# Attention and a gated feed-forward on one core: the planner's DMA account, the fillers' rule, a third score buffer and a fixed draw

## The chip, the cores and the metric

The kernel runs on one core of a Trainium2 chip. A core has five engines with an instruction stream of their own, which runs in order: TensorE (PE, matrix products; its weight loads show as PEld), VectorE (DVE), ScalarE (ACT), GpSimd (POOL) and SyncE (SP, which here only starts DMA transfers). The metric is the device time of one execution in microseconds (us). Three timed runs of the kernel before gave 817.39 us in the median, 816.01 to 819.08.

## The reference

Four sequences of 448 tokens, 12 heads of width 64, fp32. Scores are mixed over heads before the softmax and the attention weights after it; what comes out goes, per token, through a layer of 768 to 2048 to 768 with the gate h * clip(h + 3, 0, 6) / 6.

```python
scores = scale * np.matmul(q, k.transpose(0, 1, 3, 2))
scores = np.einsum('bhij,hg->bgij', scores, w_pre)
scores = scores - np.max(scores, axis=-1, keepdims=True)
attn = np.exp(scores)
attn = attn / (np.sum(attn, axis=-1, keepdims=True) + 1e-09)
attn = np.einsum('bhij,hg->bgij', attn, w_post)
out = np.matmul(attn, v)                     # then x: (1792, 768)
h = x @ w_in
g = h * np.clip(h + 3.0, 0.0, 6.0) / 6.0
y = g @ w_out
```

## The kernel before

The queries of one sequence are taken in blocks m of 60 (8 blocks in each of 4 sequences, 32 in all). For a block, `scores` (L433) multiplies queries and keys of two head pairs at a time, three times (p = 0, 1, 2), each into a pair of PSUM banks. ACT copies the result to a buffer `s` in SBUF (L458; in the first two blocks ACT and DVE copy a half each, L455 and L456), and SP sends each `s` in four transfers (L465) to the tile T, where heads lie on partitions. T has two homes, `T_two` and `T_one`, for even and odd blocks.

`step` takes 10 queries in each of two halves from T: `pre` (L522, mixing over heads before the softmax) on PE, the row maximum `nb` on DVE (L530), the exponential on ACT (L531), the division on POOL (L540) and `post` (L559, mixing over heads after the softmax) on PE, whose result ACT and DVE put into `AR` (L570, L568). From step 24 on `post` works in split f16 (`eh`, `el`, L542, L543), before that in fp32 (the x32 and x64 rows). `av` (L604) multiplies AR by the values. `moe1` (L802) is the first product of the layer, with weights `wi` that DVE, ACT and POOL decode from 64-bit words (`w_in_item`, L650 to L720); the second product (L1076) is computed with seven block products P1 to P7 and runs from 618 us to the end. L840 are fillers: products of the identity that nobody reads.

No order is written by hand. The builder lists every piece of work with an engine, a duration, what it needs and a priority, and `Plan.schedule` plays it through on a modelled machine: each engine takes the ready piece of the lowest priority, PE staying with its kind of product for up to `stay`. What comes out is emitted as the static order of each engine. A transfer's landing is modelled by one rate (`DMA_RATE`) and a fixed lag. The priorities are shaken in 32 draws, with four values of `stay` each, and the plan with the earliest modelled end is taken. `filler` is asked at each PE piece with the modelled gap before it, and fills the gap with identity products while the modelled time is between 9 and 150.

Of the kernel before, what the change touches and what calls it, by code (L numbers as in the profile page):

```python
# [11 lines left out]
F16 = mybir.dt.float16  # L12
BF16 = mybir.dt.bfloat16
# [13 lines left out]
P = 128  # L27
# [4 lines left out]
CU = 60  # L32
# [27 lines left out]
TRIALS, JITTER = 32, 0.3  # L60


class Op:
    __slots__ = ("eng", "dur", "fn", "prio", "n", "succ", "order", "ready", "end", "bytes", "no", "mode", "takes", "then", "share")
# [49 lines left out]
class Plan:  # L114
# [3 lines left out]
    DMA_RATE = 345e3  # L118
# [3 lines left out]
    STAY = 3.0, 4.0, 6.0, 8.0  # L122
# [5 lines left out]
    def op(self, eng, dur, fn, r=(), w=(), prio=0.0, after=(), nbytes=0, mode=0, share=False):  # L128
        o = Op()
        o.share = share or eng == "POOL"  # L130
# [46 lines left out]
    def schedule(self, prio, stay):  # L177

        free, wait, ready, out = {}, {}, {}, []
        bw, mode, then = {"SP": 0.0, "ACT": 0.0}, None, None  # L180
        for o, n in zip(self.ops, self.counts):
            o.n, o.ready, o.end = n, 0.0, None
# [31 lines left out]
        while True:  # L214
# [19 lines left out]
            if e == "PE":  # L234
# [6 lines left out]
                o = x[2]  # L241
                for b in o.takes:
                    b.pool.take(b, self.HOP)
# [10 lines left out]
            if e == "PE" and self.filler:  # L254
                z = self.filler(free[e], t)
                if z is not None:
                    out.append((free[e], z))
# [18 lines left out]
    def run(self):  # L276
        self.link()
        best = None
        for k in range(TRIALS):
# [12 lines left out]
def body(ctx: ExitStack, tc: tile.TileContext, q4, kT, vj, wpre0, wpost0, ident0, w_in, w_out, outT):  # L292
# [37 lines left out]
    def pe(dur, fn, r, w, prio, after=(), mode=0):  # L330
        return plan.op("PE", dur, fn, r, w, prio, after, 0, mode)
# [7 lines left out]
    def bulk(nbytes, out, src, w, prio, after=()):  # L339
        q = BULK  # L340
        return plan.op(q, 0.5 if q == "SP" else 0.4, lambda: (SP if q == "SP" else ACT).dma_start(out(), src), [], w, prio, after, nbytes)
# [20 lines left out]
    def across(src, name, prio):  # L362

        slot = place(singles)
        top = const([1, 1], BF16, f"top_{name}")
# [10 lines left out]
    wpre0_f, wpre8 = (const([P, 64], F32, n, one) for n in ("wpre0_f", "wpre8"))  # L376
    wpost0_f, wpost_n = (const([P, HR], F32, n, one) for n in ("wpost0_f", "wpost_n"))
# [3 lines left out]
    def mixes():  # L381
        dma(32768, lambda: SP.dma_start(wpre0_f(), wpre0), [], [wpre0_f], -11)
        dma(30720, lambda: SP.dma_start(wpost0_f(), wpost0), [], [wpost0_f], -10.9)
        dma(32768, lambda: SP.dma_start(ident(), ident0), [], [ident], -10.8)
        pool(0.2, lambda: POOL.memset(ones(), 1.0), [], [ones], -20)
        dve(0.2, lambda: DVE.tensor_scalar(wpre8(), wpre0_f(), 1.0 / 8.0, None, op0=ALU.mult), [wpre0_f], [wpre8], -6)
        dve(0.3, lambda: amax(wst(), wpost0_f()), [wpost0_f], [wst], -6)
        wm, wmv = across(wst, "w", -5.5)

        def fin():  # L390
            pow2(wmv(), pw(), rw())
            DVE.tensor_scalar(wpost_n(), wpost0_f(), rw(), 2.0 ** 14, op0=ALU.mult, op1=ALU.mult)
# [3 lines left out]
        dve(1.0, fin, [(wm, 1), wpost0_f], [pw, rw, wpost_n, wpost_h, wpost_l], -3)  # L396
# [17 lines left out]
    AR = const([P, 17280], F16, "AR", apool)  # L414
    T_two = const([P, 6144], F16, "T_two", apool)
    T_one = const([P, 6, S], F32, "T_one", one)
    T_home = [lambda: T_two()[:, :5376].bitcast(F32).rearrange("p (t j) -> p t j", t=6), T_one]
# [4 lines left out]
    def a_view():  # L422
        return AR()[:, :].bitcast(F32).rearrange("p (x y) -> p x y", y=3 * CU)
# [13 lines left out]
    def scores(m, p, at):  # L437
# [7 lines left out]
        st = buf(wpool, [P, 2, S], F32, "x", f"s_{m}_{p}", X_BUFS) if m == 0 else buf(rot, [P, 2, S], F32, "s", f"s_{m}_{p}", 2)  # L445
# [750 lines left out]
```

## Time and profile before

| | |
|---|---|
| median of three runs | 817.39 us (816.01 to 819.08) |
| profiled execution | 814.55 us, of which the span is 812.6 us |
| busy PE, DVE, ACT, POOL | 97%, 74%, 65%, 46% of the span |
| fillers (L840) | 98 products |
| granted TensorE clock, mean | 0.994 |

A busy PE is not a PE at its peak: matmuls overlap, and a row of mean 259 ns may start every 96 ns. So what PE has to do is read from blocks of instructions in order of time (so many products from start to start) and what it loses from the gaps. The clock is given as a share of full speed: 1.0 is 2.4 GHz, 0.5 is 1.2 GHz.

### The profile page before, as it was taken

How to read it: one execution, taken by the hardware profiler on the slowest of the kernel's cores; microseconds unless marked ns; L12 is line 12 of the kernel's file. 1: busy time of each engine (PE TensorE's matmuls, PEld its weight loads, DVE VectorE, ACT ScalarE, POOL GpSimd, SP SyncE). 2: the span in 40 equal slices, each digit the busy share in tenths (PEclk: the TensorE clock that was granted, in tenths of full speed). 3: DMA queues.
4: the chain of work that ended last, by engine and by line, in shares of the span. 5: the costliest groups of instructions: out<-in, count | busy, mean ns of one | idle time of the engine just before them, and what ended most of it. 6: DMA issues, size and time to landing. Idle time of an engine off the chain costs nothing.

```text
span 812.6 us, 28101 instructions
## 1 busy us (share of the span) xinstructions
PE 791.4 (97%) x11634; PEld 639.0 (79%) x11634; DVE 599.9 (74%) x1185; ACT 529.6 (65%) x1043; POOL 376.7 (46%) x535
## 2 busy tenths in 40 slices
PE   8999988999999999999999998999999999999998
PEld 3466676577767788777786776678999999999998
DVE  4589898687669656987946888875479889888632
ACT  2477887778898767788767687885469584233200
POOL 3255799567789626677753676774310000000000
PEclk9799999999999999999999999999999999999999
DMA  6756671664455476667446855745459992754101
GB/s 217 235 162 210 186 232 54 191 219 144 142 153 177 121 247 214 201 196 243 137 151 213 274 170 178 223 123 180 139 169 363 339 329 72 226 154 143 35 19 52
DMA packets 100415, 146.96 MB, mean 181 GB/s; under 512 B 9824, under 2 KB 79552, under 8 KB 100288
## 3 DMA queue, kind: packets, MB, share of 16 engines
q1 hardware_dynamic: 100288, 145.17, 57.2%
q8 instruction: 91, 1.49, 0.8%
q14 instruction: 36, 0.29, 0.1%
HBM read 75.23 MB, written 31.20 MB: 131 GB/s over the span
## 4 chain that ended last, share of the span: by engine, by line
PE 62%; DMA 9%; ACT 8%; POOL 6%; DVE 6%; SPq 5%; issue 3%; ACTq 0%; POOLq 0%; DVEq 0%
PE single L1076 24%; PE single L802 16%; PE single L559 6%; PE pair L433 5%; SPq L465 4%; PE single L522 4%; PE single L604 4%; ACT e L531 3%; POOL el L543 2%; POOL e L540 2%; DMA T_two<-s 2%; PE single L840 2%; DMA wi<-in_w_in 2%; ACT s L458 2%; DMA wo<-in_w_out 2%
## 5 line engine op out<-in xcount | busy, mean ns | idle before, releaser
L802 PEld LDWEIGHTS <-wi 128*128 128x128 f16 x2304 | 213.0, 98 | 22.7 <-issue 14.1
L802 PE MATMUL single<-x,wi 128*128 128x208 f16 (+1 forms) x2304 | 227.6, 259 | 2.8 <-ACT e L531 2.2
L543 POOL TENSOR_TENSOR el<-e,eh 128x448 f16<-128x448 f32 x156 | 176.0, 1145 | 36.6 <-ACT eh L542 33.3
L540 POOL TENSOR_SCALAR e<-e,r 128x448 f32<-128x448 f32 x180 | 131.2, 739 | 34.0 <-DVE r L534 29.1
L1076 PEld LDWEIGHTS <-ws_P 128*128 128x128 f16 x1440 | 138.0, 98 | 0.0
L531 ACT ACTIVATE e<-single,nb 128x448 f32<-128x448 f32 x180 | 113.0, 636 | 22.7 <-DVE nb L530 22.6
L530 DVE TENSOR_REDUCE nb<-single 128x1 f32<-128x448 f32 x180 | 102.0, 614 | 17.7 <-PE single L522 17.1
L542 ACT ACTIVATE eh<-e 128x448 f16<-128x448 f32 x156 | 87.5, 579 | 23.5 <-POOL e L540 23.0
L458 ACT ACTIVATE s<-pair 128x896 f32<-128x896 f32 x90 | 82.4, 916 | 21.3 <-DMA T_two<-s 6.7
L433 PE MATMUL pair<-ks,qx 64*64 64x448 f32 x728 | 89.3, 560 | 3.7 <-ACT s L458 3.2
L815 ACT ACTIVATE g<-single,three,uh 128x208 f32<-128x208 f32 (+1 forms) x128 | 68.7, 539 | 37.1 <-PE single L802 35.5
L817 DVE SCALAR_TENSOR_TENSOR g<-g,six,single 128x208 f32<-128x208 f32 (+1 forms) x128 | 56.4, 442 | 44.8 <-ACT g L815 42.9
L604 PEld LDWEIGHTS single<-AR,v 128*64 128x64 f32 x1536 | 75.1, 137 | 13.4 <-issue 3.4
L559 PEld LDWEIGHTS <-eh 60*128 60x128 f16 x2496 | 66.5, 100 | 20.9 <-issue 19.5
L604 PE MATMUL single<-AR,v 128*64 128x120 f32 (+1 forms) x1536 | 80.4, 263 | 0.4 <-ACT e L531 0.4
L559 PE MATMUL single<-wpost_h,el 60*128 60x60 f16 x1248 | 72.4, 202 | 1.9 <-POOL el L543 1.9
L559 PE MATMUL single<-wpost_h,eh 60*128 60x60 f16 x1248 | 72.9, 202 | 0.5 <-DVE g L817 0.4
L559 PE MATMUL single<-wpost_l,eh 60*128 60x60 f16 x1248 | 72.5, 202 | 0.0
L533 POOL TENSOR_SCALAR sm<-sm 128x2 f32<-128x2 f32 (+1 forms) x92 | 21.8, 237 | 106.3 <-ACT e L531 101.4
L1076 PE MATMUL single<-gx_P,ws_P 128*128 128x224 f16 x720 | 69.3, 259 | 0.0
L559 PEld LDWEIGHTS <-el 60*128 60x128 f16 x1248 | 64.1, 101 | 2.5 <-POOL el L543 2.4
L568 DVE TENSOR_SCALAR AR<-single 128x480 f32<-128x480 f32 (+1 forms) x92 | 58.1, 639 | 9.6 <-PE single L559 9.2
(247 smaller groups left out, 1176.9 us busy)
## 6 DMA issues: line engine op xcount, KB each, us to landing
T_two<-s SPq DMA_DIRECT2D x192, 105.0 KB
T_one<-s SPq DMA_DIRECT2D x144, 105.0 KB
wi<-in_w_in SPq DMA_DIRECT2D x16, 768.0 KB
wo<-in_w_out SPq DMA_DIRECT2D x24, 512.0 KB
wsd_P<-WF SPq DMA_DIRECT2D x42, 256.0 KB
wP<-wsd_P SPq DMA_DIRECT2D x36, 256.0 KB
gd<-g SPq DMA_DIRECT2D x32, 240.0 KB
gd<-g SPq DMA_DIRECT2D x32, 208.0 KB
```

The costliest lines, as they stand in the source:

```text
L433: PE.matmul(at[u]()[cc * D:cc * D + D], q()[r, o:o + D], ks_[cc]()[r, pr % 3, :], start=True, stop=True)
L458: act(0.9, lambda: ACT.activation(st(), two()[:, :, :S], AF.Copy), ps, [(st, 0), (st, 1)], at + 0.5)
L530: dve(0.53, lambda r=r: DVE.tensor_reduce(nb()[:, r:r + 1], ps[r]()[:, :S], axis=AX.X, op=ALU.max, negate=True), [ps[r]], [(nb, r)], s + 0 ...
L531: act(0.62, lambda r=r: ACT.activation(e()[:, r], ps[r]()[:, :S], AF.Exp, bias=nb()[:, r:r + 1], accum_out=sm()[:, r:r + 1]), [ps[r], (nb, ...
L540: pool(0.63, lambda r=r: POOL.tensor_scalar(e()[:, r], e()[:, r], rr()[:, r:r + 1], 1.0, op0=ALU.mult, op1=ALU.mult), [rr], [(e, r)], s + ...
L542: act(0.47, lambda r=r: ACT.activation(eh()[:, r], e()[:, r], AF.Copy), [(e, r)], [(eh, r)], s + 0.65 + 0.3 * r)
L543: pool(1.02, lambda r=r: POOL.tensor_tensor(el()[:, r], e()[:, r], eh()[:, r], op=ALU.subtract), [(e, r), (eh, r)], [(el, r)], s + 0.7 + 0 ...
L559: PE.matmul(out, x()[rows, r, js], z()[rows], start=(i == 0), stop=(i == len(mix) - 1))
L604: PE.matmul(ps()[u * D:(u + 1) * D, k:k + (n if p1 else CI)], v()[:, jc, g * D:(g + 1) * D], cols(jc * H + g), start=(jc == 0), stop=(jc = ...
L802: PE.matmul(pv(), wi_g[g]()[:, w, f0, cc, :], x()[:, z, cc, :n], start=(cc == 0 and i == 0), stop=(cc == 5 and i == 2))
L815: act(0.44, lambda fc=fc, pv=pv, r=r: ACT.activation(r(), pv(), AF.Relu, bias=three()[:, fc:fc + 1], scale=uh()[:, fc:fc + 1]), [ps, (thre ...
L1076: PE.matmul(ps()[:, :NH], w_view(w, y, 2 * m + i)[:, f], g(x)[:, f, :], start=(i == 0 and f == 0 and (y, x) == (0, 0)), stop=(i == 1 and f ...
```

## The change

- Scores on their way out. The ring of `s` has three places in place of two (`S_BUFS`). In the first two blocks the transfers of the half that DVE copied (u = 1) are issued by ACT, the others by SP; so 12 of 24 go to ACT's stream.
- The planner's transfers. The rate is 302e3 in place of 345e3 bytes per us; a transfer starts 1.1 after its issue begins; the lag behind it is 1.0, or 2.0 for scores and 3.0 for bulk loads (it was 1.9 for all); a score transfer is charged as 184 kB and 0.77 of issue (126 kB and 0.8).
- Fillers. `filler` now also adds up the modelled streaming time in the last `SPAN` before the end of the piece to come, and where it is under `LEAST` (half) of it adds further identity products, which push that piece back in the model. There are 129 fillers in place of 98.
- The draw. One draw (6) and one `stay` (8.0) in place of 32 times 4.
- Room. Some small tiles share places; `T_two` is 5376 wide and `AR` 17664, and the split weights of P1 lie in AR rather than in T_two: their splitting comes after the last `av` (`a_last`), while the first pieces of g, now in T_two, come after the last `pre` (`t_last`).

No other instruction is added or taken away; by the new plan all of them stand in another order. The diff, cut to its core:

```diff
-TRIALS, JITTER = 32, 0.3
+DRAWS, JITTER = (6,), 0.3
+S_BUFS, LAT_T, LAT_B = 3, 2.0, 3.0
...
-    DMA_RATE = 345e3
+    DMA_RATE = 302e3
-    STAY = 3.0, 4.0, 6.0, 8.0
+    STAY = (8.0,)
+    FILL, SPAN, LEAST = 0.215, 3.41, 0.5
...
+                n, fn, z = fill
+                if fn is not None:
+                    out.append((free[e], fn))
+                o.end += z
+                recent.append((free[e], t + z, self.FILL * n))
+                recent.append((t + z, o.end, o.st))
...
-                x, d, other = max(bw[e], o.end + 0.6), o.bytes / self.DMA_RATE, "ACT" if e == "SP" else "SP"
+                x, d, other = max(bw[e], t + 1.1), o.bytes / self.DMA_RATE, "ACT" if e == "SP" else "SP"
-                o.end = bw[e] + 1.9
+                o.end = bw[e] + o.lat
...
-        for k in range(TRIALS):
+        for k in DRAWS:
...
-    T_two = const([P, 6144], F16, "T_two", apool)
+    T_two = const([P, 5376], F16, "T_two", apool)
...
-        st = buf(wpool, [P, 2, S], F32, "x", f"s_{m}_{p}", X_BUFS) if m == 0 else buf(rot, [P, 2, S], F32, "s", f"s_{m}_{p}", 2)
+        st = buf(wpool, [P, 2, S], F32, "x", f"s_{m}_{p}", X_BUFS) if m == 0 else buf(rot, [P, 2, S], F32, "s", f"s_{m}_{p}", S_BUFS)
...
-                        SP.dma_start(T()[4 + h:4 + h + 12 * (r - 1) + 1:12, t0:t0 + t], st()[D * cc + q0:D * cc + q0 + r * t, u, :])
+                        (ACT if m < 2 and u else SP).dma_start(T()[4 + h:4 + h + 12 * (r - 1) + 1:12, t0:t0 + t], st()[D * cc + q0:D * cc + q0 + r * t, u, :])
-                    plan.op("SP", 0.8, go, [(st, u), T_zero[m % 2]], [(T, (h, t0))], at + 0.7, (), r * t * 2100)
+                    plan.op("ACT" if m < 2 and u else "SP", 0.77, go, [(st, u), T_zero[m % 2]], [(T, (h, t0))], at + 0.7, (), t * 30700, lat=LAT_T)
...
+        n = int((t1 - at[0]) / 0.22 + 2.5) if t1 - at[0] >= 0.1 else 0
+        a = t1 + o.dur - plan.SPAN
+        have = sum(st * (min(1.0, (y - a) / (y - x)) if y > x else 0.0) for x, y, st in recent if y > a) + min(n * plan.FILL, t1 - at[0]) + o.st
+        short = plan.LEAST * plan.SPAN - have
+        more = int(short / plan.FILL + 0.9) if short > 0.0 else 0
...
-            w_split("P1", i, t, PRE_AT + i + 0.5, t_last)
+            w_split("P1", i, t, PRE_AT + i + 0.5, a_last)
```

The stream of SP near the start, behind the loads of keys and queries; `s_0_1` is block 0, p = 1, `v` and `wi` are loads of values and weights. Before:

```order
L341 DMA wi_0_118<-in_w_in 128x768
L465 DMA T_two_105<-s_0_0_125 10x6x448 x4
L465 DMA T_two_105<-s_0_1_140 10x6x448 x4
L465 DMA T_two_105<-s_0_2_159 10x6x448 x4
L465 DMA T_one_96<-s_1_0_167 10x6x448 x4
L465 DMA T_one_96<-s_1_1_187 10x6x448 x4
L341 DMA v_0_299<-in_vj 128x768 x2
L465 DMA T_one_96<-s_1_2_304 10x6x448 x3
L341 DMA v_0_299<-in_vj 128x768
```

After:

```order
L350 DMA wi_0_118<-in_w_in 128x768
L475 DMA T_two_100<-s_0_0_127 10x6x448 x2
L475 DMA T_two_100<-s_0_1_155 10x6x448 x2
L475 DMA T_two_100<-s_0_2_182 10x6x448 x2
L475 DMA T_one_109<-s_1_0_185 10x6x448 x2
L350 DMA qx_0_2_204<-in_q4 128x724
L475 DMA T_one_109<-s_1_1_206 10x6x448 x2
L475 DMA T_one_109<-s_1_2_209 10x6x448 x2
L350 DMA v_0_257<-in_vj 128x768
```

SP has half the score transfers left, and the last of block 1 stands ahead of the values.

The stream of ACT near the start, up to the decoding of the first weights. Before, from the second copy:

```order
L455 ACTIVATE s_0_0_125<-pair0_120 128x448
L455 ACTIVATE s_0_1_140<-single0_85 128x448
L455 ACTIVATE s_0_2_159<-single3_146 128x448
L455 ACTIVATE s_1_0_167<-single5_153 128x448
L455 ACTIVATE s_1_1_187<-single1_129 128x448
L650 ACTIVATE WF_189<-wi_0_118 128x768
L713 ACTIVATE wi_0_240<-WF_189,wir_0_227 128x768
```

After, from behind the first copy:

```order
L475 DMA T_two_100<-s_0_0_127 10x6x448 x2
L465 ACTIVATE s_0_1_155<-single1_149 128x448
L475 DMA T_two_100<-s_0_1_155 10x6x448 x2
L465 ACTIVATE s_0_2_182<-single3_163 128x448
L465 ACTIVATE s_1_0_185<-single5_171 128x448
L475 DMA T_two_100<-s_0_2_182 10x6x448 x2
L475 DMA T_one_109<-s_1_0_185 10x6x448 x2
L465 ACTIVATE s_1_1_206<-single1_149 128x448
L465 ACTIVATE s_1_2_209<-single3_163 128x448
L475 DMA T_one_109<-s_1_1_206 10x6x448 x2
L475 DMA T_one_109<-s_1_2_209 10x6x448 x2
L661 ACTIVATE WF_251<-wi_0_118 128x768
```

Twelve transfers stand between the copies, ahead of the decoding (`WF`); the copy of `s_1_2` has come up from between the first exponentials.

The stream of PE around the last `av`; L569 is `post`, L614 is `av`, L378 and L380 pass a maximum across partitions. Before:

```order
L802 LDWEIGHTS wi_1_1746
L802 MATMUL single4_148<-x_6_9448,wi_1_1746 128x240
L604 MATMUL single0_85<-AR_366,v_3_8570 64x90 x24
L604 MATMUL single3_146<-AR_366,v_3_8570 64x90 x24
L370 LDWEIGHTS ones_114
L370 MATMUL single1_129<-top_wo0_11307,ones_114 128x1
```

After:

```order
L569 LDWEIGHTS el_179_11339
L569 MATMUL single2_151<-wpost_h_145,el_179_11339 128x60
L378 LDWEIGHTS wo_m_1_11249
L378 MATMUL single1_149<-ident_105,wo_m_1_11249 1x128
L378 LDWEIGHTS wo_m_0_11276
L378 MATMUL single4_165<-ident_105,wo_m_0_11276 1x128
L614 MATMUL single0_85<-AR_352,v_3_8493 64x90 x24
L614 MATMUL single5_171<-AR_352,v_3_8493 64x90 x24
L380 LDWEIGHTS ones_96
L380 MATMUL single1_149<-top_wo1_11448,ones_96 128x1
```

The product of the layer that stood ahead of the last `av` is gone from there; the last `post` is now two small products ahead of it.

## Rows read from the trace of the kernel before

**Rows 1.** The page: span; busy time of the engines.
```profile
span 812.6 us, 28101 instructions
...
PE 791.4 (97%) x11634; PEld 639.0 (79%) x11634; DVE 599.9 (74%) x1185; ACT 529.6 (65%) x1043; POOL 376.7 (46%) x535
```

**Rows 2.** Busy time by stretch: length, then each engine (its instructions), clock, DMA, GB/s.
```profile
0.00:45.00 45.00, 40.42 (x307) 19.59 (x307) 22.91 (x52) 18.41 (x39) 14.05 (x26) 0.89 0.70 224
45.00:126.00 81.00, 77.48 (x1109) 53.94 (x1108) 73.52 (x170) 65.45 (x128) 57.55 (x92) 1.00 0.61 189
126.00:170.00 44.00, 41.69 (x659) 25.47 (x656) 31.96 (x64) 32.56 (x64) 31.84 (x49) 1.00 0.48 145
170.00:400.00 230.00, 228.03 (x4044) 176.46 (x4041) 175.67 (x380) 185.72 (x400) 159.22 (x219) 1.00 0.60 185
400.00:520.00 120.00, 114.95 (x2023) 86.67 (x2022) 87.26 (x181) 88.81 (x195) 73.31 (x95) 1.00 0.64 195
618.00:812.60 194.60, 191.54 (x2000) 191.28 (x1997) 141.87 (x199) 72.51 (x92) 0.00 (x0) 1.00 0.52 165
```

**Rows 3.** Fillers alone, by the same view.
```profile
45.00:126.00 81.00, 5.01 (x20) 1.00 0.61 189
80.00:100.00 20.00, 2.12 (x9) 1.00 0.63 193
126.00:170.00 44.00, 9.19 (x37) 1.00 0.48 145
```

**Rows 4.** Instructions in order, TensorE from the start: start, duration, line, operands, count.
```profile
16.79 5.35 PE L840 MATMUL single<-ident 128*128 128x512 bf16 x24
22.07 1.74 PE L522 MATMUL single<-T_two,wpre 64*64 64x448 f32 x16
...
26.83 5.97 PE L559 MATMUL single<-wpost_n,e 60*128 60x60 f32 x64 [0.72 <-POOL e L540]
...
39.03 0.92 PE L433 MATMUL pair<-ks,qx 64*64 64x448 f32 x8
39.89 2.00 PE L559 MATMUL single<-wpost_n,e 60*128 60x60 f32 x32
```

**Rows 5.** The same for the DMA queue of SyncE.
```profile
6.91 10.55 SPq L465 DMA_DIRECT2D T_two<-s  x12
...
29.23 0.77 SPq L465 DMA_DIRECT2D T_one<-s  x1
```

**Rows 6.** The same for ScalarE.
```profile
6.34 0.54 ACT L455 ACTIVATE s<-pair 128x448 f32<-128x448 f32 x1 [4.33 <-PE pair L433]
...
13.41 0.89 ACT L650 ACTIVATE WF<-wi 128x768 f32<-128x768 f32 x1 [1.96 <-DMA wi<-in_w_in]
...
23.75 0.63 ACT L531 ACTIVATE e<-single,nb 128x448 f32<-128x448 f32 x1 [4.09 <-DVE nb L530]
```

**Rows 7.** The same for VectorE.
```profile
43.58 1.16 DVE L530 TENSOR_REDUCE nb<-single 128x1 f32<-128x448 f32 x2 [0.46 <-PE single L522]
```

**Rows 8.** Groups of instructions by line: busy, mean ns.
```profile
L714 DVE SCALAR_TENSOR_TENSOR wi<-WF,wir,wi 128x768 f16<-128x768 f32 x4 | 4.5, 1116 | 2.4 <-ACT wi L713 2.4
```

**Rows 9.** Two short stretches, busy time: the first 10 us, the half clock.
```profile
0.00:10.00 10.00, 8.23 (x48) 2.80 (x52) 2.49 (x7) 3.02 (x5) 4.94 (x7) 1.00 0.83 280
28.00:38.00 10.00, 10.00 (x69) 6.06 (x71) 4.12 (x6) 3.00 (x6) 2.65 (x5) 0.50 0.79 257
```

**Rows 10.** The chain of waits from 80 us: start, duration, what.
```profile
85.24 4.41 DMA T_one<-s
...
93.08 4.60 DMA T_two<-s
```

**Rows 11.** The chain of waits from 405 us.
```profile
414.91 2.02 DMA T_one<-s
...
489.29 3.99 DMA T_two<-s
```

**Rows 12.** Waits summed: us, times, longest.
```profile
PEld single L604 <- ACT AR L570: 1.4, 2, 0.7
```

More of the change, by code (lines that the diff above doesn't have):

```diff
@@ L1 @@
+import collections
 import heapq
@@ L59 @@
 NH = S // 2
-TRIALS, JITTER = 32, 0.3
+DRAWS, JITTER = (6,), 0.3
+S_BUFS, LAT_T, LAT_B = 3, 2.0, 3.0
 class Op:
-    __slots__ = ("eng", "dur", "fn", "prio", "n", "succ", "order", "ready", "end", "bytes", "no", "mode", "takes", "then", "share")
+    __slots__ = ("eng", "dur", "fn", "prio", "n", "succ", "order", "ready", "end", "bytes", "no", "mode", "takes", "then", "share", "lat", "st")
 class Buf:
@@ L126, in __init__, with op @@
         self.ops, self.bufs, self.filler = [], {}, None
-    def op(self, eng, dur, fn, r=(), w=(), prio=0.0, after=(), nbytes=0, mode=0, share=False):
+    def op(self, eng, dur, fn, r=(), w=(), prio=0.0, after=(), nbytes=0, mode=0, share=False, lat=1.0, st=None):
         o = Op()
+        o.lat, o.st = lat, dur if st is None else st
         o.share = share or eng == "POOL"
@@ L241, in schedule @@
                 o = x[2]
+                fill = self.filler(free[e], t, recent, o) if self.filler else (0, None, 0.0)
                 for b in o.takes:
@@ L253, in schedule @@
                 port[e] = o.end
[L254 to L257, printed above, removed]
+            if e == "PE":
+                n, fn, z = fill
[4 more added lines that the diff above has]
+                recent.append((t + z, o.end, o.st))
             if e == "PE":
@@ L340, in bulk @@
         q = BULK
-        return plan.op(q, 0.5 if q == "SP" else 0.4, lambda: (SP if q == "SP" else ACT).dma_start(out(), src), [], w, prio, after, nbytes)
+        return plan.op(q, 0.5 if q == "SP" else 0.4, lambda: (SP if q == "SP" else ACT).dma_start(out(), src), [], w, prio, after, nbytes, lat=LAT_B)
     def amax(dst, src):
@@ L373, in body @@
     F = [b * STEPS + 12 * c for b in range(B) for c in range(4)]
[L376 to L377 removed]
+    wpre8 = const([P, 64], F32, "wpre8", one)
+    wpost_n = const([P, HR], F32, "wpost_n", one)
     wpost_h, wpost_l = (const([P, HR], F16, n, one) for n in ("wpost_h", "wpost_l"))
@@ L559, in post @@
                             PE.matmul(out, x()[rows, r, js], z()[rows], start=(i == 0), stop=(i == len(mix) - 1))
-        pe(dur * R, post, [x for x, _ in mix] + [z for _, z in mix], [*po, (a, (t, 2))], s + 1.2, mode=2)
+        pe(dur * R, post, [x for x, _ in mix] + [z for _, z in mix], [*po, (a, (t, 2))], s + 1.2, mode=2, st=0.38 * R if s < POST16 else 0.3 * R)
         far = G5 * R
@@ L830, in body, with filler @@
         PE.matmul(singles.makes[0]()[:, :], warm[:, :P], warm, start=True, stop=True)
-    def filler(t0, t1):
-        n = int((t1 - t0) / 0.22 + 2.5)
-        free = [i for i in range(len(singles.held)) if (singles.free_at(i, 0.3) or (0 if singles.held[i] is None else 1e9)) <= t0]
-        if t0 < FILL_FROM or t0 > FILL_TO or t1 - t0 < 0.1 or not free:
-            return None
+    def filler(t0, t1, recent, o):
+        if t0 < FILL_FROM or t0 > FILL_TO:
+            return 0, None, 0.0
+        at = [singles.free_at(i, 0.2) if singles.held[i] is not None else 0.0 for i in range(len(singles.held))]
+        at = min(((max(x, t0), i) for i, x in enumerate(at) if x is not None), default=None)
+        if at is None or at[0] > t1:
+            return 0, None, 0.0
+        n = int((t1 - at[0]) / 0.22 + 2.5) if t1 - at[0] >= 0.1 else 0
[3 more added lines that the diff above has]
+        more = int(short / plan.FILL + 0.9) if short > 0.0 else 0
         def fn():
-            for _ in range(n):
-                PE.matmul(singles.makes[free[0]]()[:, :].rearrange("p (a b) -> p a b", a=4), ident(),
+            for _ in range(n + more):
+                PE.matmul(singles.makes[at[1]]()[:, :].rearrange("p (a b) -> p a b", a=4), ident(),
                           ident().unsqueeze(1).broadcast_to([P, 4, P]), start=True, stop=True)
-        return fn
+        return n + more, fn if n + more else None, more * plan.FILL
     plan.filler = filler
```

39 lines of the change are left out of this document (21 added, 18 removed).

## The prediction

> **What bounds the kernel now.** I read the page first: PE is busy 97% of the span, the next engine 74% [rows 1]. Then busy time by stretch, which shows three regimes [rows 2]. From 618 us on PE streams the second product without a gap until 3.06 us before the end (191.54 of 194.60). From 170 to 618 it is full but for small gaps: 1.97 us in 170 to 400, but 5.05 in 400 to 520. Before 170 it is not the bound. In 45 to 126 VectorE is busy 73.52 of 81 us, and PE's 77.48 hold fillers [rows 3]. Up to 45 us VectorE is busy 22.91 only and the granted clock averages 0.89: there everybody waits for the first scores. So the time is PE's work (the same in both kernels) plus what PE loses: gaps, fillers, and half clock. The gaps come to 812.6 - 791.4 = 21.2 us. A change of order can only touch these losses, most of them before 170 us.
>
> The first loss in order of time: SP issues the twelve transfers of block 0 back to back, 10.55 us, 0.88 each, and the last of block 1 starts at 29.23 [rows 5]; PE bridges with fillers to the first `pre` at 22.07 [rows 4], and the first exponential comes at 23.75 [rows 6]. Then the clock falls to 0.5 [rows 9]: in the 10 us before it PE had done fillers, three `pre` and little else. Thirty-two records of `post` take 2.00 us at full clock, so 64 should take 4.0 and took 5.97 [rows 4]; about 10 us at half clock cost some 5.
>
> **The change part by part, against the profiled execution of 814.55 us** (span 812.6; it lies 2.84 under the median of 817.39, and I carry that difference to the end).
>
> A, the start: the split of the first transfers, and fillers that hold the clock. I walk the new order with old durations. ACT: its first copy starts at 6.34; six copies of 0.54 are 3.2 [rows 6]. Twelve transfers issued by ACT are in no row; from SP 0.88 each, so 10.6; from below nothing; from above 1.8 each, 21.6, if each also waits for an earlier transfer (the fifth rival). I take SP's price, the only row. With 0.6 for the wait for DVE's first copy and 0.89 for the decoding behind them ACT is free at 6.3 + 3.2 + 10.6 + 0.6 + 0.9 = 21.6, where the first exponential was at 23.75. SP: the fourth of its six transfers of block 0 needs a completion slot of the weights' load, which lands at about 13.4 [rows 6]; three at 0.88 from there end at 16.0; in time for PE. PE: the last products of block 1 wait for ACT's third copy, at 6.3 + 3 x 0.54 + 0.6 + 4 x 0.88 = 12.0; with two products of 0.92 and what waits between I put their end at 14.5; 27 fillers at 0.22 (5.35 for 24 [rows 4]) are 6.0; the first `pre` starts at 20.5, 1.6 earlier than 22.07. From there the order has three `pre` of 0.76 (2.3), 28 products of filler or score up to the first `post` (9 + 5 fillers, half a score product: 3.5), then until the sixth `pre`: three `post` of 1.93 (5.8), two score products (1.8), four fillers (0.9), three `pre` (2.3). That is 37.1, and the twelfth maximum is done 0.6 later, at 37.7; before it was 43.58 + 1.16 = 44.7 [rows 7]. Seven us earlier; five of them are the half clock. But VectorE then still owes seven instructions that it had behind it before: one of 1.12 [rows 8] and six small ones, 2.2 in all, because the first weights are decoded later. As VectorE is the bound from there on, A is worth 7 - 2 = 5. Bounds: 7.2 gained, and 6 lost by the fifth rival.
>
> B, three places for `s`. The chain of waits passes through a copy of ACT that waits for transfers of older scores: 4.41 and 4.60 us at 85 and 93 us [rows 10], 2.02 and 3.99 at 415 and 489 [rows 11]. With a third place the copy waits for transfers three scores back. PE's loss where these stand: the gap of 5.05 in 400 to 520 [rows 2], and in 80 to 100 its 2.12 of fillers [rows 3] and about 1 of gap: 8.2 at most. If 400 to 520 lost what 170 to 400 loses (0.9%), it would lose 1.0. That is the nearest row, so 4. Below nothing: 2 to the bad, since every queue's order is new and SP starts other loads earlier. What is late next there: the load of values and SP's own queue.
>
> C, 31 more fillers. Nine of them stand in the walk of A already; behind it the order has 79, before 57: 22 x 0.22 = 4.8 if each one pushes real work back, 0 if they stand in gaps. Up to 170 us PE has 3.52 + 2.31 of gaps outside them [rows 2], in the stretches where they go; gaps can take 5.8. I take 1.
>
> D, the end of attention. The last `av` has lost the layer's product in front of it, so it meets the last `post` directly, and waits for its eviction: `av` behind that eviction waited up to 0.7 [rows 12], the eviction itself takes about as long; 1. P1's six weight splits move behind that `av`, the three pieces of g ahead; ACT is busy 72.51 of 194.60 after 618 and 25 us of layer work separate them from the first use, so 0; without that cover 6 x 0.7 = 4.
>
> Planner's costs, draw and smaller tiles have no cost of their own: they are the order that A to D read.
>
> Sum: -5 - 4 + 1 + 1 = -7, so 807.5 profiled, and with 2.84 a median of 810.
>
> Two rules of the Trainium skill speak against parts of it. The trace shows 280 GB/s and a DMA share of 0.83 in the first 10 us [rows 9], so transfers may be held by the loads, not by issuing. DMA: Bandwidth & Descriptors, "Issuing engines are not separate DMA queues", says that transfers started from several engines run on the same DMA engines and interleave, and that only the sequencer's issue time is saved. By it the second rival below holds; the row agrees for the first 10 us alone.
>
> The trace shows one fall of the clock, at 28 us, and none after it. TensorE: Matmul & The Clock Gate, "Loop structure matters more than you think", has waits between matmuls as what makes PE run cold; it does not say that a filler count worked out beforehand suffices. By it the fourth rival can hold; this trace has no run with other fillers.
>
> **The rivals.**
>
> 1. All of it works: A 7.2, B 8.2, C and D nothing. For: VectorE's debt can be paid in its remaining gaps (81 - 73.52 = 7.5). Against: loads of values stay in the chain. -15.4: 802.
> 2. The first transfers land no earlier. For: loads fill the DMA engines up to 10 us. Against: after that SP's issuing sets the pace. The first `pre` then stays at 22.07, A is the clock's 5 less the debt, 3: 812.
> 3. Nothing is kept: A and B are eaten by the bounds behind them (VectorE to 126 us, POOL and ACT at 31.84 and 32.56 of 44 us to 170 [rows 2]). For: both are near full there. Against: work comes earlier to all of them. 817.
> 4. The change does not do what it says: the clock still falls once in the start. That costs 5 again: 815.
> 5. Slower: ACT's stream. Its copies, exponentials and evictions stand behind twelve issues, and each of these may first wait for an earlier transfer's completion. Every 0.1 us more per issue moves A's walk by 1.2. From 0.88 + 5 / 12 = 1.3 each A is gone, from 0.88 + 7 / 12 = 1.46 the sum is, and at 1.8 A is -5 + 11 = +6: 814.55 + 6 - 4 + 1 + 1 = 818.5, a median of 821; at 2.0 each, 824. For: nothing in the trace has ACT issue a transfer. Against: on SP, which waits for the same completions, 12 take 10.55.
>
> **How the numbers follow.** Chances: forecast 0.40 (804 to 815 by itself), rival one 0.20, two 0.09, three 0.15, four 0.05, five 0.11. The range leaves a tenth out on each side: from just under the first rival, 801, to halfway between the third and the fifth, 819. This kernel's measurement tells 0.5%, 4.1 us, from no change, so faster means under 813.3. That is nearly all of the forecast (0.37), the first rival, most of the second (0.06) and a little of the others (0.02): 0.65. Same (813.3 to 821.5): the rest of the forecast, of the second and fourth, most of the third and a part of the fifth: 0.22. Slower: 0.13.
>
> **What would show it.** A: the first `pre` near 20.5, the first exponential near 21.6, granted clock 1.0 from its first rise to the end, the twelfth maximum near 38. B: no copy of `s` in the chain that waits for a transfer, and PE's gap in 400 to 520 near 1. C: gaps before 170 us smaller by about what the fillers grew. D: a gap of about 1 at the last `av`, then none until the end. The prediction is wrong if VectorE's stretch does not start earlier (A), if another transfer takes the place of the scores in the chain (B), or if ACT's issues cost over 1.46 us each.

## The result and the profile after

The kernel after took 808.02 us (median of six runs, 803.26 to 811.29), the kernel before in the same comparison 816.14 (814.29 to 819.08). The ratio is 0.9898, with a 95% interval of 0.9862 to 0.9935: 8.1 us faster by medians. The profiled execution of after is the fastest of its six, 803.26 us; so a comparison of the two profiles (814.55 to 803.26, 11.3) shows some 3 us more than the medians do.

The page after, which answers to [rows 1]:

```profile
span 801.2 us, 28170 instructions
...
PE 787.7 (98%) x11665; PEld 639.6 (80%) x11665; DVE 596.2 (74%) x1185; ACT 529.5 (66%) x1043; POOL 377.4 (47%) x535
```

The gaps of PE fell from 21.2 us to 801.2 - 787.7 = 13.5. PE's busy time fell too, by 3.7, though it holds 31.46 us of fillers (129) and before it held 24.80 (98). So the span's 11.4 is: gaps -7.7, fillers +6.7, and the products of the work itself -10.4 (766.6 to 756.2 us of records, the same number of instructions). Of the last, about 5 is the half clock that is gone (the prediction's estimate, from a row at either level). The other 5.4 is spread over `scores`, `pre`, `post` and `av`, whose records come out shorter in sum; since the ends of matmuls are modelled, I can't say from a trace which of these records had held a stall.

Busy time by stretch, after (columns as in [rows 2]: length, PE, PEld, DVE, ACT, POOL, granted clock, DMA share, GB/s):

```profile
0.00:45.00 45.00, 42.20 (x355) 19.61 (x355) 24.45 (x56) 21.53 (x44) 15.96 (x27) 1.00 0.72 239
45.00:126.00 81.00, 80.81 (x1117) 55.75 (x1114) 73.79 (x164) 62.82 (x121) 59.60 (x94) 1.00 0.55 176
126.00:170.00 44.00, 42.99 (x775) 27.44 (x773) 30.96 (x73) 38.91 (x81) 37.60 (x60) 1.00 0.61 190
170.00:400.00 230.00, 226.04 (x4068) 176.22 (x4069) 172.83 (x378) 186.56 (x403) 164.57 (x223) 1.00 0.58 179
400.00:520.00 120.00, 118.87 (x2036) 94.00 (x2034) 84.94 (x182) 88.55 (x189) 69.67 (x92) 1.00 0.64 196
570.00:580.00 10.00, 8.74 (x203) 7.89 (x202) 5.17 (x19) 3.61 (x8) 3.27 (x6) 1.00 0.63 201
...
580.00:798.00 218.00, 218.00 (x2293) 217.41 (x2290) 163.41 (x240) 92.97 (x126) 0.81 (x5) 1.00 0.56 178
```

Against [rows 2]: the granted clock of the first stretch is 1.00 (0.89 before); the gap in 400 to 520 is 1.13 us (5.05), in 45 to 126 it is 0.19 (3.52). In 170 to 400 it grew from 1.97 to 3.96. The fillers alone, by the same view, beside [rows 3]:

```profile
0.00:45.00 45.00, 14.37 (x61) 5.53 (x61) 1.00 0.72 239
45.00:126.00 81.00, 11.31 (x46) 3.92 (x47) 1.00 0.55 176
126.00:170.00 44.00, 5.78 (x23) 1.73 (x21) 1.00 0.61 190
```

The start, PE in order of time (L858 is the filler, L532 `pre`, L569 `post`; compare [rows 4]):

```profile
14.14 6.00 PE L858 MATMUL single<-ident 128*128 128x512 bf16 x27
20.07 2.49 PE L532 MATMUL single<-T_two,wpre 64*64 64x448 f32 x24
...
26.92 2.00 PE L569 MATMUL single<-wpost_n,e 60*128 60x60 f32 x32
...
36.25 1.69 PE L532 MATMUL single<-T_one,wpre 64*64 64x448 f32 x16
```

The first `pre` starts at 20.07 (predicted 20.5), the 32 products of `post` take 2.00 each time, and the sixth `pre` is done at 37.9 (37.1). ScalarE and its DMA queue, beside [rows 6] (ACTq is the queue; L475 the transfers, L661 the decoding, L541 the exponential):

```profile
7.72 2.20 ACTq L475 DMA_DIRECT2D T_two<-s  x2
...
10.11 1.60 ACTq L475 DMA_DIRECT2D T_two<-s  x2
...
18.01 3.16 ACTq L475 DMA_DIRECT2D T_one<-s  x3
21.21 0.92 ACT L661 ACTIVATE WF<-wi 128x768 f32<-128x768 f32 x1 [3.66 <-DMA T_one<-s]
22.02 0.62 ACT L541 ACTIVATE e<-single,nb 128x448 f32<-128x448 f32 x1
```

An issue takes ScalarE 0.78 us in the median and 1.38 at its worst, the first; the twelve take 11.6 with the short waits between them, 0.96 each, under the 1.3 from which A would have been gone by the fifth rival. The first exponential is at 22.02 (predicted 21.6). VectorE, beside [rows 7] (L540 takes the maxima, L353 a maximum over a load of values):

```profile
36.85 0.94 DVE L353 TENSOR_REDUCE vst<-v 128x1 f32<-128x768 f32 x1
...
38.24 0.94 DVE L353 TENSOR_REDUCE vst<-v 128x1 f32<-128x768 f32 x1
...
39.89 1.13 DVE L540 TENSOR_REDUCE nb<-single 128x1 f32<-128x448 f32 x2
```

The twelfth maximum is done at 41.0, not 37.7: the order puts two reductions of values and smaller work of the weights between the maxima. Of these 3.3 us, 0.8 are `pre` itself, the rest is VectorE. It is 3.7 us earlier than before, where 7 less a debt of 2 had been forecast.

In the chain of waits (start, duration, what) score transfers have become rarer: behind the first 45 us they stand in it seven times before, for 25.8 us in all, and four times after, for 8.8. The longest transfer in it is now the one load of values, which stays, as the first rival said:

```profile
72.28 2.42 DMA T_one<-s
...
419.49 3.22 DMA T_one<-s
...
439.08 7.19 DMA v<-in_vj
```

It is not new; the chain before has it too:

```profile
454.11 7.01 DMA v<-in_vj
```

And ScalarE's copies of `s` that wait for a transfer (us in total, times, longest), first before, then after:

```profile
ACT s L458 <- DMA T_two<-s: 6.7, 5, 2.3
ACT s L458 <- DMA T_one<-s: 4.1, 5, 2.0
```

```profile
ACT s L465 <- DMA T_one<-s: 3.8, 1, 3.8
...
ACT s L468 <- DMA T_two<-s: 1.6, 2, 1.1
```

From the third block on (L458 before, L468 after) these waits fall from 10.8 us to 2.0 (the 1.6 and 0.4 more for T_one). The 3.8 stands in the first two blocks, where ScalarE's copy now follows its own issues.

The end of attention, PE in order of time:

```profile
572.85 0.20 PE L569 MATMUL single<-wpost_h,el 60*128 60x60 f16 x2 [0.34 <-POOL el L553]
...
573.92 3.94 PE L614 MATMUL single<-AR,v 128*64 128x90 f32 x96 [0.42 <-DVE AR L578]
577.79 0.20 PE L380 MATMUL single<-top_wo,ones 1*128 1x1 bf16 x2
...
579.58 4.62 PE L813 MATMUL single<-x,wi 128*128 128x208 f16 x50 [0.50 <-DVE x L620]
```

Waits of 0.34, 0.42 and 0.50 surround the last `av`; from 580 to 798 PE has no gap.

So far nearly everything looks as forecast. But the profile of one order can't say whether the parts that changed brought the time, or the order that they led to. The experiments ask that.

### The profile page after: what moved, and what is told of

It is laid out like the page before. It is cut to its first block, busy times and chain, and to the rows that moved or that the text cites. A ratio compares the mean times of both kernels' runs of the same rounds, so it can differ in the third digit from the quotient of the medians.

```text
span 801.2 us, 28170 instructions
## 1 busy us (share of the span) xinstructions
PE 787.7 (98%) x11665; PEld 639.6 (80%) x11665; DVE 596.2 (74%) x1185; ACT 529.5 (66%) x1043; POOL 377.4 (47%) x535
## 4 chain that ended last, share of the span: by engine, by line
PE 78%; DMA 6%; POOL 4%; ACT 4%; DVE 4%; SPq 2%; issue 2%; ACTq 0%; DVEq 0%
PE single L1094 24%; PE single L813 22%; PE single L569 9%; PE pair L443 7%; PE single L532 6%; PE single L614 6%; PE single L858 3%; SPq L475 2%; POOL el L553 2%; DMA wsd_P<-WF 2%; DMA T_one<-s 1%; POOL e L550 1%; ACT e L541 1%; DMA v<-in_vj 1%; DMA wi<-in_w_in 1%
## 5 line engine op out<-in xcount | busy, mean ns | idle before, releaser
L553 POOL TENSOR_TENSOR el<-e,eh 128x448 f16<-128x448 f32 x156 | 172.0, 1121 | 39.0 <-ACT eh L552 34.0
L550 POOL TENSOR_SCALAR e<-e,r 128x448 f32<-128x448 f32 x180 | 129.0, 728 | 37.8 <-DVE r L544 29.8
L541 ACT ACTIVATE e<-single,nb 128x448 f32<-128x448 f32 x180 | 113.4, 639 | 16.1 <-DVE nb L540 16.0
L540 DVE TENSOR_REDUCE nb<-single 128x1 f32<-128x448 f32 x180 | 102.1, 614 | 17.7 <-PE single L532 17.3
L826 ACT ACTIVATE g<-single,three,uh 128x240 f32<-128x240 f32 (+1 forms) x128 | 69.4, 542 | 41.9 <-PE single L813 39.8
L468 ACT ACTIVATE s<-pair 128x896 f32<-128x896 f32 x90 | 82.7, 919 | 15.2 <-PE pair L443 10.8
L828 DVE SCALAR_TENSOR_TENSOR g<-g,six,single 128x240 f32<-128x240 f32 (+1 forms) x128 | 56.6, 443 | 48.0 <-ACT g L826 47.3
L614 PEld LDWEIGHTS single<-AR,v 128*64 128x64 f32 x1536 | 75.2, 137 | 10.2 <-ACT eh L552 3.8
L569 PEld LDWEIGHTS <-eh 60*128 60x128 f16 x2496 | 66.2, 100 | 17.5 <-issue 14.3
L614 PE MATMUL single<-AR,v 128*64 128x120 f32 (+1 forms) x1536 | 78.7, 262 | 0.7 <-DVE AR L578 0.4
L543 POOL TENSOR_SCALAR sm<-sm 128x2 f32<-128x2 f32 (+1 forms) x92 | 26.2, 285 | 111.9 <-ACT e L541 107.4
L569 PE MATMUL single<-wpost_h,el 60*128 60x60 f16 x1248 | 71.9, 202 | 1.3 <-POOL el L553 1.3
L569 PE MATMUL single<-wpost_h,eh 60*128 60x60 f16 x1248 | 71.8, 202 | 0.0
L569 PE MATMUL single<-wpost_l,eh 60*128 60x60 f16 x1248 | 71.7, 202 | 0.0
L580 ACT ACTIVATE AR<-single 128x480 f32<-128x480 f32 (+1 forms) x92 | 53.2, 582 | 20.8 <-PE single L569 20.8
```

Source lines behind the costliest of these rows:

```text
L468: act(0.9, lambda: ACT.activation(st(), two()[:, :, :S], AF.Copy), ps, [(st, 0), (st, 1)], at + 0.5)
L540: dve(0.53, lambda r=r: DVE.tensor_reduce(nb()[:, r:r + 1], ps[r]()[:, :S], axis=AX.X, op=ALU.max, negate=True), [ps[r]], [(nb, r)], s + 0 ...
L541: act(0.62, lambda r=r: ACT.activation(e()[:, r], ps[r]()[:, :S], AF.Exp, bias=nb()[:, r:r + 1], accum_out=sm()[:, r:r + 1]), [ps[r], (nb, ...
L550: pool(0.63, lambda r=r: POOL.tensor_scalar(e()[:, r], e()[:, r], rr()[:, r:r + 1], 1.0, op0=ALU.mult, op1=ALU.mult), [rr], [(e, r)], s + ...
L553: pool(1.02, lambda r=r: POOL.tensor_tensor(el()[:, r], e()[:, r], eh()[:, r], op=ALU.subtract), [(e, r), (eh, r)], [(el, r)], s + 0.7 + 0 ...
L569: PE.matmul(out, x()[rows, r, js], z()[rows], start=(i == 0), stop=(i == len(mix) - 1))
```

## Experiments

Ratios are to the kernel before on the same chip. Three chips were used, and on one chip the medians compare directly: two_places, two_planned_three_places, no_least and all_on_sp; before_filled, draw_0, draw_1 and earlier_start; the last four. After itself was not among any of these three groups, so it is compared with them by its ratio.

**The third place: with two, planned anew, and with two planned and three given.**

```diff
-S_BUFS, LAT_T, LAT_B = 3, 2.0, 3.0
+S_BUFS, LAT_T, LAT_B = 2, 2.0, 3.0
```

> The changed kernel with two places for the scores, planned anew with draw 6. If the third place carries term B, PE's gap in 400 to 520 us comes back (5.05 before, 1.13 after) and the ratio to the kernel before is about 0.995 (some 812 us). If the planner's account and the draw carry it, the ratio stays at 0.990 (808).

The second run keeps this order and gives the ring a third tile that the planner doesn't know of:

```diff
-        return Buf(lambda: pool.tile(shape, dt, tag=tag, name=name, bufs=bufs), g)
+        real = 3 if tag == "s" else bufs
+        return Buf(lambda: pool.tile(shape, dt, tag=tag, name=name, bufs=real), g)
```

> The same order of every engine as in the run with two places, but three tiles in the ring. If the place itself is what helps, this is 3 to 5 us faster than the run with two places, and copies of scores no longer wait for transfers. If only an order made for three places helps, it is the same within 1 us.

Measured: two_places 820.79, ratio 1.0072 (1.0044 to 1.0099); two_planned_three_places 817.03, ratio 1.0001 (0.9978 to 1.0023). So neither branch of the first expectation held: two places came out slower than the kernel before, not at 0.995 or 0.990. Both spend 33.45 us on 135 fillers. The stretch 400 to 520, first with two places, then with three:

```profile
400.00:520.00 120.00, 116.15 (x1972) 90.47 (x1971) 83.08 (x180) 89.13 (x192) 72.19 (x95) 0.99 0.61 189
```

```profile
400.00:520.00 120.00, 117.83 (x2087) 91.39 (x2089) 86.90 (x185) 90.64 (x195) 73.61 (x97) 1.00 0.63 196
```

The 0.99 of the first line is a fall of the clock from 412.5 to 415.9 us. ScalarE's copies of pairs wait for transfers 11.0 us in all with two places (5.7 and 5.3), 3.1 with three. So in one and the same order the third place is worth 3.8 us by medians, the size that was given to B. But this order with three places is no faster than the kernel before, and after, with three places by its plan, is 1% faster: that percent is in the order itself.

**The half rule for fillers: the changed order without the eleven that it adds.**

```diff
-            for _ in range(n + more):
+            for _ in range(n):
```

> The changed kernel in the same order, without the 11 fillers (2.4 us) that the half-of-the-stretch rule adds; the other 118 stay. If they hold the clock, it falls in the first 60 us as before and the time is 3 to 5 us longer (811 to 813). If they only stand in the way, the clock stays at 1.0 and the time is 1 to 2.4 us shorter (806).

Measured: 804.16, ratio 0.9853 (0.982 to 0.9886), the lowest of all runs. The granted clock stays 1.0 from 4 us to the end without them. So the half rule isn't what holds the clock in this order, and its fillers cost something between nothing and some 4 us (0.9898 against 0.9853, intervals that overlap). The rule accounts for eleven of the 31 additional fillers. The other twenty come with the new order and with a part of the change not named above: `filler` may now use a bank that comes free inside the gap, where before it had to be free when the gap began. No run separates these two.

**The split of the first transfers: the changed order with all of them on SP.**

```diff
-                        (ACT if m < 2 and u else SP).dma_start(T()[4 + h:...
+                        SP.dma_start(T()[4 + h:...
```

> The changed kernel with the 24 first score transfers all issued by SP, everything else in the same order. If SP's issuing sets the start, the first pre moves from 20.1 to 22 us or later, the first T_one pre from 34.7 to 36 or later, and the time is 2 to 4 us longer (810 to 812). If the loads set it, the first pre stays near 20 and the time is the same; and since ACT loses 12 issues, its first exponential comes earlier than 22.0.

Measured: 808.85, ratio 0.9906 (0.9877 to 0.9935). PE's start:

```profile
14.26 6.00 PE L858 MATMUL single<-ident 128*128 128x512 bf16 x27
20.19 2.49 PE L532 MATMUL single<-T_two,wpre 64*64 64x448 f32 x24
```

The first `pre` starts 0.12 us later than with the split, behind the same 27 fillers, and the twelfth maximum is done at 40.96 (41.02 with it). The split is worth nothing that can be measured. It does bring transfers out sooner: the last of block 1 is issued at 21.89 with it and at 26.93 without, and by the semaphore updates in the traces the last of block 0 completes at 18.2 and 19.2 us (before: 20.7). But nothing waits for them: in both runs PE is still at its fillers, to 20.1 and 20.3. So it is PE's own stream, not the landing, that sets the first `pre` here, as the prediction's walk had it. That agrees with the rule of the Trainium skill that the prediction weighed (DMA: Bandwidth & Descriptors, "Issuing engines are not separate DMA queues"): another issuing engine saves issue time alone.

**Is it the fillers that set the first `pre`? Fewer of them, and only block 0 split.**

```diff
-                        (ACT if m < 2 and u else SP).dma_start(T()[4 + h:...
+                        (ACT if m < 1 and u else SP).dma_start(T()[4 + h:...
...
-            for _ in range(n + more):
+            for _ in range(12 if n > 20 else n):
```

The second edit takes out the half rule's fillers as well.

> The changed kernel in its order with three edits: no fillers from the half rule, 12 in place of 27 fillers ahead of the first pre, and only block 0's transfers split between SP and ACT. If PE's own fillers and ACT's issues set the first pre and the first exponential, and not the landing, they come at 17 to 18 and 18 to 19 us in place of 20.1 and 22.0, and the time is 2 to 3 us under the run without the half rule (ratio 0.982). If the transfers set it, the first pre waits for them until about 20 and the ratio is 0.985 as without the half rule; if the clock falls for want of fillers, it is 0.990 or more.

Measured: 806.49, ratio 0.9876 (0.9839 to 0.9913).

```profile
14.82 2.76 PE L858 MATMUL single<-ident 128*128 128x512 bf16 x12
20.47 4.11 PE L532 MATMUL single<-T_two,wpre 64*64 64x448 f32 x24 [2.89 <-DMA T_one<-s]
```

With 12 fillers PE waits 2.89 us for a transfer and starts `pre` at 20.47 all the same: in this run the transfers set that moment. But they came later than in after. Block 0's issues, in the queue that issues its last (count; least, median and longest duration in ns; start of the first and of the last), in earlier_start, then after, then all_on_sp:

```profile
L475 ACTq DMA_DIRECT2D T_two<-s x6: 778/778/1371, 8.4 to 16.1; - x6
```

```profile
L475 ACTq DMA_DIRECT2D T_two<-s x6: 778/778/1377, 7.7 to 14.1; - x6
```

```profile
L475 SPq DMA_DIRECT2D T_two<-s x12: 748/748/967, 7.2 to 16.5; - x12
```

The last completes at 20.0 us here, at 18.2 in after. So how early `pre` could start in after with fewer fillers isn't settled: there the 27 end some 2 us behind the landing. In the wait the granted clock fell (20.4 to 23.8), and the 24 products took 4.11 in place of 2.49. So the long row of fillers also covers the clock. Its removal doesn't show in the time: the ratio lies between those of all_on_sp and no_least.

**The half clock alone: the order before, with 12 fillers ahead of its first `post`.**

```diff
+            if s == 0:
+                for _ in range(12):
+                    PE.matmul(po[0]()[:, :].rearrange("p (a b) -> p a b", a=4), ident(),
+                              ident().unsqueeze(1).broadcast_to([P, 4, P]), start=True, stop=True)
```

> The kernel before in its order, with 12 more fillers (2.6 us) between its first three pre and the first post, where PE waited. If what PE did ahead of 28 us made the clock fall, it stays at 1.0 and, 5 us of half clock less about 1.5 us of fillers that do not fit the wait, the time is 3 us shorter or more (ratio 0.996). If VectorE's stretch takes the rest, the ratio is 1.000; if the fall has another cause, the clock falls all the same and the ratio is 1.002.

Measured: 819.26, ratio 1.0036 (1.0008 to 1.0065). PE from there (L563 is `post`, L844 the filler, L522 `pre`):

```profile
28.45 3.79 PE L563 MATMUL single<-wpost_n,e 60*128 60x60 f32 x64
...
45.03 1.22 PE L844 MATMUL single<-ident 128*128 128x512 bf16 x3 [0.83 <-ACT AR L574]
...
46.38 2.31 PE L844 MATMUL single<-ident 128*128 128x512 bf16 x5
```

The 64 products take 3.79 in place of 5.97 [rows 4]: the fall at 28 is gone. Another comes instead behind a short wait, 45.3 to 48.7 (five fillers take 2.31, nearly twice their usual 1.25). The twelfth maximum is done at 41.5, 3.2 us sooner than before, and none of that is left in the time. The rule of the Trainium skill on waits between matmuls (TensorE: Matmul & The Clock Gate, "Loop structure matters more than you think") makes long waits for a transfer what lets PE run cold. The 2.89 us of earlier_start fit it; here a wait of 0.83 for ScalarE stands ahead of the fall, and covering one wait left the next one open. The twelve fillers also take 2.76 us of PE, so this run doesn't give the price of the clock alone; it shows that A's five can't be had by holding the clock at 28 us and by an earlier twelfth maximum.

**The draw: the changed kernel with other draws.** All its rules stay; only the seed of the priorities' noise changes.

```diff
-DRAWS, JITTER = (6,), 0.3
+DRAWS, JITTER = (0,), 0.3
```

> The changed kernel planned without any shaking of the priorities (draw 0), all else as changed. If the account, the fillers' rule and the third place are what helps, the ratio to the kernel before is within 0.005 of the changed kernel's 0.990. If draw 6 was the lucky one, it is 0.998 or more.

> The same with draw 1. Two draws near 0.990 say that the draw matters little; two at 0.998 or more say that the draw carries most of the gain; one of each leaves a spread of draws as wide as the gain.

Measured: draw_0 834.09, ratio 1.0203 (1.0153 to 1.0252); draw_1 829.24, ratio 1.0153 (1.011 to 1.0195). With every rule of the change in place, both are slower than the kernel before. Draw 0 starts much as after does (28 fillers ahead of the first `pre` where after has 27), 2.5 us later, with a fall of the clock at 8.7 to 12.1. The larger loss comes later, with three places for `s`:

```profile
400.00:520.00 120.00, 115.45 (x1995) 90.93 (x1994) 90.20 (x187) 88.10 (x194) 72.31 (x95) 1.00 0.64 198
520.00:600.00 80.00, 73.12 (x1330) 59.51 (x1324) 48.13 (x106) 50.82 (x111) 44.40 (x63) 0.94 0.45 136
```

A gap of 4.55 in 400 to 520, nearly that of the kernel before, and 6.88 in 520 to 600, where the clock falls from 589 to 599; two more falls stand at 172.5 and 199.8. Draw 1 has its largest gaps later: 11.8 us from 600 us on.

**What makes a draw good?** Here the planner's own number helps. It is not a measurement: as the program is built, the planner computes the end of the order by its account, and this end can be read for any draw. Draw 6 has the lowest of draws 0 to 159 at this `stay` (798.6); the middle one has 809.7, and draws 0 and 1 are in the worst fifth (815.6 and 820.1). Four runs ask whether that ranking is real.

```diff
-DRAWS, JITTER = (6,), 0.3
+DRAWS, JITTER = (35,), 0.3
```

> The changed kernel with draw 35 in place of 6. The planner computes an end for each draw while it builds the program: 798.6 for draw 6, 815.6 and 820.1 for draws 0 and 1, and 798.9 for draw 35. Theory 'the account ranks the draws' (a draw counts by the end that the new account gives it): as the changed kernel, 805 to 812 us, ratio to before 0.985 to 0.995, gaps of some 1 to 2 us of TensorE in 400 to 520. Rival 'draw 6 is a lucky one' (draws differ on the chip in ways the account doesn't see): between the other draws measured, 815 to 834 us, ratio 1.00 to 1.02, with a gap of 4 us or more in 400 to 520 or a fall of the clock.

```diff
-    DMA_RATE = 302e3
-    STAY = (8.0,)
+    DMA_RATE = 345e3
+    STAY = (6.0,)
...
-                x, d, other = max(bw[e], t + 1.1), o.bytes / self.DMA_RATE, "ACT" if e == "SP" else "SP"
+                x, d, other = max(bw[e], o.end + 0.6), o.bytes / self.DMA_RATE, "ACT" if e == "SP" else "SP"
...
-                o.end = bw[e] + o.lat
+                o.end = bw[e] + 1.9
...
-  ... at + 0.7, (), t * 30700, lat=LAT_T)
+  ... at + 0.7, (), r * t * 2100, lat=LAT_T)
```

> The changed kernel with the old account of transfers (rate 345e3, start 0.6 behind the issue's end, lag 1.9, scores charged by 126 kB at most) and the draw that this account likes best of 32 times 4 (draw 25, stay 6, modelled end 795.0). Three places, split transfers and fillers stay. Theory 'the account ranks the draws': the old one chooses an order that needs transfers earlier than they land; 812 to 822 us, ratio 0.995 to 1.007, and ScalarE's copies of s wait longer for transfers than in the changed kernel. Rival 'three places and any good draw suffice': 804 to 811, ratio 0.985 to 0.993.

> The changed kernel with two places for s and the draw that is best with two by the new account (draw 21, stay 3, modelled end 805.4 against 807.9 for draw 6, which took 820.8 us). Theory 'the third place carries the gain': 815 to 820 us, ratio 0.999 to 1.005, TensorE loses 3 to 5 us in 400 to 520 as before. Rival 'the choice by the new account carries it, the place little': 806 to 812, ratio 0.987 to 0.995.

> The changed kernel without the half rule for fillers (LEAST 0) and the best draw without it (74 of 160, modelled end 796.7). Theory 'the account ranks the draws, and the half rule costs': 801 to 806 us, ratio 0.980 to 0.988, at or below the changed order without the eleven fillers (804.2). Rival 'within 2 us of modelled end a draw's rank says nothing': 806 to 815. Rival 'the half rule holds the clock in orders other than draw 6': the granted clock falls at least once, 3 to 4 us each.

Measured, beside the earlier runs:

| kernel | modelled end | median us | ratio (95%) |
|---|---|---|---|
| before (old account, two places, draw 7) | 797.4 | 816.14 | 1 |
| after (draw 6) | 798.6 | 808.02 | 0.9898 (0.9862 to 0.9935) |
| draw_35 | 798.9 | 807.10 | 0.9861 (0.9817 to 0.9904) |
| no_half_draw_74 | 796.7 | 809.95 | 0.9893 (0.9851 to 0.9934) |
| draw_0 | 815.6 | 834.09 | 1.0203 (1.0153 to 1.0252) |
| draw_1 | 820.1 | 829.24 | 1.0153 (1.011 to 1.0195) |
| two_places (draw 6) | 807.9 | 820.79 | 1.0072 (1.0044 to 1.0099) |
| two_places_best (draw 21) | 805.4 | 813.89 | 0.9958 (0.9929 to 0.9988) |
| old_account_best (draw 25) | 795.0 | 824.21 | 1.0085 (1.0048 to 1.0122) |

Draw 6 is not a lucky one: draw 35, which the account rates the same, takes the same. The old account's favourite, with three places, split transfers and the half rule all in, has the lowest modelled end and took 16 to 17 us more than draw_35 on the same chip, a little more than the 822 that its theory allowed. It has 85 fillers, since they too are placed by the modelled gaps. By the new account chip and model differ by 8 to 19 us and rank 799 against 816 rightly; by the old one they differ by 19 and 29. The new one does not tell orders apart that it rates within 5 us (draw_74 is modelled 2 better than draw 6 and is no faster, so its theory missed; 0 and 1 come in the wrong order). two_places_best, at 0.9958, lies between its two branches; the 6.5 us that the account rates it behind draw 35 are what was measured, 6.8. draw_74 also kept the half rule's question open: its clock did fall once, 10 to 14 us, without the rule, but draw_35 has a fall at 8 to 12 with it.

Where old_account_best shows a part of its loss, busy time by stretch and a wait of PE (first it, then draw_35 for the stretch):

```profile
170.00:400.00 230.00, 220.01 (x3880) 168.75 (x3878) 168.46 (x372) 179.69 (x386) 163.16 (x222) 0.99 0.55 167
```

```profile
PE pair L443 <- ACT s L468: 4.7, 5, 1.7
```

```profile
170.00:400.00 230.00, 226.82 (x4123) 173.98 (x4122) 178.17 (x387) 191.60 (x412) 169.55 (x232) 1.00 0.58 178
```

A gap of 9.99 against 3.18, and score products that wait 4.7 us for ScalarE's copies in the whole run, 2.6 of them in this stretch; in draw_35 PE has no such wait. The copies themselves wait 4.5 between 170 and 520 for score transfers, against 1.1 in draw_35. That is the direction in which an account that lands transfers too soon would err, but it explains 2.6 of the 6.8 by which the gaps differ. Its profiled run was the fastest of ten (816.38), 12 us behind that of draw_35; where the rest goes is open.

The third place once more: two_places_best, the best of 32 draws at four values of `stay` with two places, is 6.8 us slower than draw_35 on the same chip. Its gap in 400 to 520 is only 1.60, though ScalarE's copies still wait 6.5 us between 170 and 520:

```profile
400.00:520.00 120.00, 118.40 (x2066) 92.46 (x2068) 92.62 (x194) 91.17 (x196) 75.52 (x94) 1.00 0.67 209
```

A good order hides most of the waits that a missing place makes; so the gap of a stretch is no measure of the place.

## Why the prediction was right, and where its reasons were not

The time was right (810 forecast, 808.02 measured), and so were most of the signs that it named. Its account of where the gain comes from was right in one term, B, and isn't borne out in another, A; that the sum came out all the same is in part luck.

- A, the start, -5. The walk held: first `pre` 20.07 for 20.5, first exponential 22.02 for 21.6, clock 1.0. Its end missed: the twelfth maximum came 3.3 late behind VectorE's reductions of values. What failed is the attribution. The split is worth nothing (0.12 us at the first `pre`): it brings the landing of block 0 from 19.2 to 18.2, and PE's fillers last until 20.1. Even in the kernel before, block 0 had landed at 20.7 and the fillers ran to 22.1, so SyncE's issuing wasn't what the first `pre` waited for. The half clock's 5 us could not be had by itself, and a twelfth maximum 3.2 us sooner brought nothing either (before_filled). And a fall isn't excluded in after either: the mean granted clock of its six runs is 1.0 twice and 0.997 or 0.998 four times, with times of 803.26 and 808.35 for the two at 1.0 and 807.08 to 811.29 for the others. So the 5 are what the clock differs by in the two profiled runs; what it gave in the medians no run shows.
- B, the third place, -4. Right in size: 3.8 us in one order, 6.8 between the best draws tried for two and for three. The gap fell to 1.13, as forecast; but two_places_best shows that this sign would have come with two places too.
- C, 31 more fillers, +1. They grew by 6.7 us of records while the gaps before 170 us fell from 10.4 to 4.0. Eleven of them cost between nothing and 4 and hold nothing in this order; +1 lies within that.
- D, +1. Measured: 0.34, 0.42 and 0.50 around the last `av`, 1.26 in 570 to 580, then no gap. Right.
- "Planner's costs, draw and smaller tiles have no cost of their own: they are the order that A to D read." This step failed. Read as a statement on one order it holds; as a reason for leaving the account out of the causes it hid one that a single pair of runs puts at 16 to 17 us. With the old account and all the rest the kernel is 0.85% slower than before; with the new account and two places 0.4% faster; with both 1.0 to 1.4% faster. So three places, the split and the half rule did not by themselves make an order fast, and of A's parts none shows by itself. Each of these cells is one or two draws, the best by its account; how much two equally rated orders of the old account differ wasn't measured, so that the old account's orders are slower as a rule is argued from one of them. The prediction got the sum since it walked the order that the account had chosen.
- The first rival (802) said that loads of values stay in the chain (7.19 us, before 7.01), and that spoke against it rightly. The second came out in that the split brings nothing, but not for its reason: transfers do land earlier, and the first `pre` came to 20.07, and to 20.19 without the split, by the new order of PE. The third, nothing kept, holds for two_planned_three_places, another order by the same rules, not for after. The fourth: the clock doesn't fall in the profiled run of after; a fall in other runs of it, and in other orders of the same rules, is what the half rule doesn't prevent. The fifth fell: 0.96 us per issue.

Open is how the 8 us divide over the stretches, beyond 400 to 520: PE's records shorten by 5.4 us that no row names.

## What to carry to other kernels

Where a planner writes the order, compare the rules of a change only at the best draw of each version, and take two draws that the model rates far apart as well: here the draws spread by 3%, three times the gain. Put the effort into the account by which orders are chosen (when does a transfer start, how long until its data can be used) before new mechanisms; a gap between modelled and measured end that differs from order to order (8 to 29 us here) is the sign. And test each mechanism inside one fixed order, where it is a clean number: 3.8 us for a place, nothing for a second issuing engine. Ask first whether anything waits for what the mechanism speeds up.

## What the runs showed of the hardware

- A score transfer's issue took ScalarE 0.78 us in the median (after; the first 1.38), about as on SyncE (0.75, all_on_sp); with the waits between them twelve took 11.6 and 10.55 [rows 5].
- Twenty-four first transfers shared by two engines were all issued by 22.6 us, by one engine by 27.7 (after, all_on_sp); the time was the same.
- The granted clock fell to half behind waits of PE as short as 0.83 us (before_filled, at 45.3). It stayed there for 3.4 us after that one (45.3 to 48.7) and after one of 2.89 (earlier_start, 20.4 to 23.8); for 10 in the kernel before (28 to 38 [rows 9]) and in draw_0, where PE had stood still for 3.23 us (589 to 599). It did not fall in the profiled run of no_least, with eleven fillers fewer.
